# Transposing the first two chunks of x with ordinary matmuls into float32 instead of transposes, and three constant matmuls behind them

## The chip, the cores and the metric

The kernel runs on one core of a Trainium2 chip. The metric is the device time of one execution in microseconds (us). A profile also gives the span, from the program's first to its last instruction on the core. In 13 of the 14 profiles below the measured time is 2.0 to 2.1 us longer than the span, so the two can be read together; the exception is named where it comes.

Engines in the profile lines: PE is TensorE's matmuls, PEld its weight loads, DVE VectorE, ACT ScalarE, SP SyncE; SPq and ACTq are the sequencers that issue transfers.

## The reference

```python
B, S, D, F = 32, 32, 1024, 3584          # all bf16
def reference(x, w_gate, w_up, w_down):
    return (gelu_tanh(x @ w_gate) * (x @ w_up)) @ w_down
```

x is 1024 tokens by 1024; the gate and up weights are 1024 by 3584; the down weight is 3584 by 1024.

## The kernel before

A helper records every operation with its dependencies, so all instructions carry one line number (L117) and one goes by tiles. The first products need x with D on the partitions, in eight chunks of 128 rows (`xT[0][:, k, :]`, 512 tokens each). Chunks 0 and 1 are loaded plainly and transposed by TensorE; chunks 2 to 7 come through the transfer engines' transposing path. Eight matmuls of ones run meanwhile, so that TensorE's clock is up when data arrives.

```python
one = nc.const_aps.tensor(1.0, [P, 512], BF16)
...                                             # ident: the 128x128 identity, bf16
for n in [512] * 6 + [P] * 2:                   # warm-up, bank 3, never read
    mm(3, one[:, 0:P], one[:, 0:n], True, True)
NX = 2                                          # chunks transposed on TensorE
for i, eng in enumerate(("sp", "act")):
    dma(eng, xn[:, 2 * i:2 * i + 2, :], x_r[:, 2 * i:2 * i + 2, 0:NX * P], 0, f"xn{i}")
for k in range(NX):
    load_first("sp", 0, k, k + 1)               # gate weights of chunk k, 128 KB
    load_first("act", 1, k, k + 1)              # up weights
for k0, k1 in ((2, 3), (3, 4), (4, 5), (5, 6), (6, 8)):
    load_x(0, k0, k1)                           # transposing transfer of x, on SP's queue
for k in range(2, 4):
    load_first("act", 0, k, k + 1)
    load_first("act", 1, k, k + 1)
act(warm[:, 0:1], const0, GELU, 0)
for k in range(NX):
    for i, b in enumerate((6, 7) if k == 0 else (4, 5)):
        half = ps[:, b, 0:P].bitcast(BF16)
        for t in range(2):
            pr.add("pe", "transpose", half[:, t * P:(t + 1) * P], xn[:, 2 * i + t, k * P:(k + 1) * P], ident[:, :])
        pr.add("dve", "tensor_copy", xT[0][:, k, i * 256:(i + 1) * 256], half)
...
steps = [(m, j, k) for k in range(DK - KO) for j in range(2) for m in range(4)]   # 8 matmuls a chunk
...
    op = mm(2 * m + j, first[:, j, k, m * P:(m + 1) * P], xT[0][:, k, :], k == 0, k in (3, DK - 1), add=k > 3)
```

Each chunk feeds eight matmuls of 512 columns: four with gate weights, then four with up weights. "The first real matmul" below is the first of chunk 0; the 17th is the first that needs chunk 2. The first GELU on a result runs at about 16 us.

## Time and profile before

| | before |
|---|---|
| time, median of the first 3 runs | 273.2 us (272.43 to 273.35) |
| span of the profiled run | 271.2 us |
| TensorE busy | 267.6 us, 99% |
| first real matmul | 4.61 us |
| slow stretch: 512-column matmuls 0.43 us apart | until 6.3 us; 0.216 us apart afterwards |

The page's engine row and its chain that ended last:

```profile
PE 267.6 (99%) x1197; PEld 191.8 (71%) x1206; DVE 203.5 (75%) x238; ACT 132.8 (49%) x213; POOL 37.2 (14%) x23
...
PE 99%; issue 0%; DVE 0%
PE ps L117 99%; DVE o L117 0%
```

TensorE hardly rests after its start, so whatever the head loses or wins reaches the end. The timeline of the head, TensorE (start us, duration us, engine, line, operation, out<-in, shape, count):

```profile
0.77 2.93 PE L117 MATMUL ps<-const-bfloat16-1.0 128*128 128x512 bf16 x8 [0.77 <-PEq L608]
3.50 1.06 PE L117 MATMUL ps<-ident,hT 128*128 128x128 bf16 x8
4.61 11.56 PE L117 MATMUL ps<-arena 128*128 128x512 bf16 x48
```

The three lines are ones, transposes (the profile calls them matmuls too) and real matmuls. Inside the second, the transposes start 0.107 us apart, the last at 4.25 us; about 0.25 us are then empty before 4.61. The copies on VectorE, from the same timeline:

```profile
3.96 0.93 DVE L117 COPY arena<-ps 128x256 bf16<-128x256 bf16 x4 [3.96 <-PE ps L117]
```

They start 0.215 us apart and take 0.29 us; the second completes chunk 0 at 4.46, and the first real matmul follows 0.15 us later.

The clock has to be read from how many matmuls fit into a microsecond. The stretches view (from:to, length, TensorE busy with the count of matmuls touched, clock column, transfer share, GB/s):

```profile
5.00:6.00 1.00, 1.00 (x4) 1.00 1.22 211
6.00:7.00 1.00, 1.00 (x6) 1.00 1.12 206
7.00:8.00 1.00, 1.00 (x6) 1.00 1.25 201
```

Busy is 1.00 in every row and the clock column says full speed, but only four matmuls touch the first stretch. The Trainium skill, "TensorE: Matmul & The Clock Gate", Part 1, explains it: TensorE starts at half clock, and a free-running activity window of about 3.4 us releases it. The trace agrees on the ratio: 0.43 us a matmul against 0.216. "Release" below means that step. Ten of the 14 traces also keep a record of the clock's steps, which the views do not show; a release given to 0.01 us is read from there. In the other four (the two of the changed kernel, `gap_xfree`, `consts_rep`) it is read from the spacing of the matmuls.

Last, the transfer of x chunk 2, issued at 2.22 us (last column: us from issue to landing):

```profile
arena<-in_x_dram SPq DMA_TRANSPOSE x1, 5.3
```

It lands at 7.54 us; the 17th matmul, which needs it, starts at 8.88. There are 1.3 us to spare here.

### The profile page before, as it was taken

How to read it: one execution, taken by the hardware profiler on the slowest of the kernel's cores; microseconds unless marked ns; L12 is line 12 of the kernel's file. 1: busy time of each engine (PE TensorE's matmuls, PEld its weight loads, DVE VectorE, ACT ScalarE, POOL GpSimd, SP SyncE). 2: the span in 40 equal slices, each digit the busy share in tenths (PEclk: the TensorE clock that was granted, in tenths of full speed). 3: DMA queues.
4: the chain of work that ended last, by engine and by line, in shares of the span. 5: the costliest groups of instructions: out<-in, count | busy, mean ns of one | idle time of the engine just before them, and what ended most of it. 6: DMA issues, size and time to landing. Idle time of an engine off the chain costs nothing.

```text
span 271.2 us, 3314 instructions
## 1 busy us (share of the span) xinstructions
PE 267.6 (99%) x1197; PEld 191.8 (71%) x1206; DVE 203.5 (75%) x238; ACT 132.8 (49%) x213; POOL 37.2 (14%) x23
## 2 busy tenths in 40 slices
PE   8999999999999999999999999999999999999996
PEld 4444448888888888888776776664458888888884
DVE  1341998998899889988764739289976999999911
ACT  2335776566756675667455564531220305067452
POOL 1000003023302330234345060000000000000000
PEclk9999999999999999999999999999999999999999
DMA  7999960050492500942900070293010000002102
GB/s 189 275 282 186 276 187 4 9 147 0 120 294 53 155 0 2 282 145 65 248 0 0 0 259 14 81 347 117 0 39 19 4 0 0 0 0 80 58 19 97
DMA packets 47039, 27.46 MB, mean 101 GB/s; under 512 B 8624, under 2 KB 47024, under 8 KB 47024
## 3 DMA queue, kind: packets, MB, share of 16 engines
q1 hardware_dynamic: 44800, 25.30, 34.4%
q10 hardware_dynamic: 2224, 1.97, 2.8%
q8 instruction: 9, 0.15, 0.2%
q14 instruction: 6, 0.05, 0.1%
HBM read 23.33 MB, written 2.10 MB: 94 GB/s over the span
## 4 chain that ended last, share of the span: by engine, by line
PE 99%; issue 0%; DVE 0%
PE ps L117 99%; DVE o L117 0%
## 5 line engine op out<-in xcount | busy, mean ns | idle before, releaser
L117 PE MATMUL ps<-S,T 128*128 128x512 f32 x560 | 129.2, 391 | 0.0
L117 PEld LDWEIGHTS ps<-S,T 128*128 128x128 f32 x560 | 105.1, 188 | 22.5
L117 ACT ACTIVATE tmp<-ps 128x512 f32<-128x512 f32 x64 | 38.0, 595 | 52.2 <-PE ps L117 52.2
L117 POOL TENSOR_TENSOR T<-arena 128x1024 fp32r<-128x1024 bf16 x17 | 36.5, 2156 | 124.4 <-PE ps L117 74.2
L117 PE MATMUL ps<-T,S 128*128 128x512 f32 x224 | 51.3, 390 | 0.0
L117 DVE TENSOR_TENSOR T<-arena,T 128x1024 fp32r<-128x1024 bf16 x42 | 50.9, 1218 | 0.2
L117 PEld LDWEIGHTS ps<-T,S 128*128 128x128 f32 x224 | 42.0, 188 | 8.8
L117 DVE TENSOR_TENSOR hT<-tmp,ps 128x512 bf16<-128x512 f32 x56 | 37.2, 684 | 14.3 <-PE ps L117 11.9
L117 ACT ACTIVATE ps<-ps 128x512 f32<-128x512 f32 x44 | 25.6, 583 | 36.6 <-PE ps L117 36.6
L117 PE MATMUL ps<-arena 128*128 128x512 bf16 x186 | 42.6, 384 | 0.4
L117 DVE TENSOR_TENSOR tmp<-ps,tmp 128x512 f32<-128x512 f32 x28 | 19.4, 692 | 23.2 <-PE ps L117 23.2
L117 PEld LDWEIGHTS ps<-arena 128*128 128x128 bf16 x192 | 17.8, 98 | 24.3 <-issue 3.2
L117 DVE TENSOR_TENSOR T<-arena 128x1024 fp32r<-128x1024 bf16 x25 | 30.0, 1220 | 5.0 <-PE ps L117 4.3
L117 DVE TENSOR_TENSOR ps<-ps,tmp 128x512 f32<-128x512 f32 x32 | 22.2, 695 | 3.0 <-PE ps L117 3.0
L117 PE MATMUL ps<-arena,hT 128*128 128x512 bf16 (+2 forms) x124 | 24.3, 355 | 0.1
L117 PEld LDWEIGHTS ps<-arena,hT 128*128 128x128 bf16 x126 | 11.7, 98 | 12.7 <-issue 0.5
L117 ACT ACTIVATE tmp<-tmp 128x512 f32<-128x512 f32 x28 | 17.6, 633 | 2.4 <-DVE tmp L117 2.1
L117 DVE TENSOR_TENSOR S<-hT 128x1024 fp32r<-128x1024 bf16 x14 | 16.6, 1219 | 0.0
L117 ACT ACTIVATE T<-arena 128x1024 fp32r<-128x1024 bf16 x14 | 14.8, 1059 | 0.0
L117 ACT ACTIVATE ps<-hT 128x512 f32<-128x512 f32 x18 | 10.7, 599 | 8.0 <-DVE hT L117 8.0
L117 ACT ACTIVATE hT<-ps 128x512 f32<-128x512 f32 x14 | 8.0, 599 | 10.8 <-PE ps L117 10.8
L117 PE MATMUL ps<-S 128*128 128x512 f32 x56 | 12.9, 389 | 0.0
(32 smaller groups left out, 89.1 us busy)
## 6 DMA issues: line engine op xcount, KB each, us to landing
arena<-in_w_down_dram SPq DMA_DIRECT2D x4, 1792.0 KB, 8.8
arena<-in_w_gate_dram SPq DMA_DIRECT2D x10, 512.0 KB, 4.0
arena<-in_w_up_dram SPq DMA_DIRECT2D x10, 512.0 KB, 5.4
out_dram<-arena SPq DMA_DIRECT2D x12, 128.0 KB, 1.7
arena<-in_w_gate_dram SPq DMA_DIRECT2D x4, 256.0 KB, 5.0
arena<-in_w_up_dram SPq DMA_DIRECT2D x4, 256.0 KB, 5.1
arena<-in_w_up_dram ACTq DMA_DIRECT2D x4, 128.0 KB, 4.0
arena<-in_w_gate_dram ACTq DMA_DIRECT2D x2, 256.0 KB, 4.0
```

The lines of the kernel that those rows point to most:

```text
L117: ins = name(eng, *args, **kw) if callable(name) else getattr(eng, name)(*args, **kw)
```

## The change

The intent is to make the head's transposes count as ordinary matmul work for the clock, and to leave TensorE no empty time while VectorE copies. The ordinary matmul writes float32 into PSUM here, so the copies now read float32.

```diff
             for i, b in enumerate((6, 7) if k == 0 else (4, 5)):
-                half = ps[:, b, 0:P].bitcast(BF16)
                 for t in range(2):
-                    pr.add("pe", "transpose", half[:, t * P:(t + 1) * P], xn[:, 2 * i + t, k * P:(k + 1) * P], ident[:, :])
-                pr.add("dve", "tensor_copy", xT[0][:, k, i * 256:(i + 1) * 256], half)
+                    pr.add("pe", "matmul", ps[:, b, t * P:(t + 1) * P], xn[:, 2 * i + t, k * P:(k + 1) * P], ident[:, :], start=True, stop=True)
+                pr.add("dve", "tensor_copy", xT[0][:, k, i * 256:(i + 1) * 256], ps[:, b, 0:256])
+        for n in range(3):
+            mm(3, one[:, 0:P], one[:, 0:P], True, True)
```

## The prediction

> **What bounds the kernel.** TensorE: busy 267.6 of 271.2 us on the page, and 99% of the chain that ended last. Any shift of the head goes one to one into the end.
>
> **The head in the timeline.** Eight matmuls of ones start at 0.77 us, 0.43 us apart (512 columns). From 3.50 the eight transposes start every 0.107 us; the last starts at 4.25. The first real matmul starts at 4.61; about 0.25 us lie idle. That start is set by VectorE: the four copies PSUM to SBUF (128x256 bf16, 0.292 us each, a new one every 0.215 us) begin at 3.96; the second, which completes x chunk 0, ends at 4.46, and 0.15 us later the matmul starts. The gate weights landed at about 4.3, before that. The real matmuls then start 0.43 us apart until 6.3 us, afterwards 0.216: the only slow-clock stretch. (The page's clock row says full speed throughout.)
>
> **What the change does.**
> 1. Transposes become ordinary 128-column matmuls. Two of the 128-column ones matmuls and the transposes show the same spacing, 0.107 us: cost 0.
> 2. The copies now read float32. The trace's 128x512 float32 copy takes 0.684 us, every 0.603; its bf16 256 copy advances 0.215. Taking one element per 0.96 GHz cycle (Trainium skill, "VectorE: DVE Perf Modes", section on PSUM operands: fp32 stays at 1x), I estimate 0.417 us each, every 0.336. Copy 2 then ends at 3.96+0.336+0.417=4.71; first real matmul at about 4.86 instead of 4.61: a loss of 0.25 us, all critical. Chunk 1 is ready at 5.4, needed after 6.5: free.
> 3. Three constant matmuls, 0.107 us each, end issue at about 4.68, inside that wait: cost 0.
> 4. The clock. Trainium skill, "TensorE: Matmul & The Clock Gate", Part 1, says a free-running activity window of about 3.4 us releases the full clock, and Part 4 that transpose mode does not count as busy the same way. In the trace the release came 5.5 us after the first matmul, with 0.86 us of transposes and 0.25 us of gap inside. If those 1.1 us count after the change, release could come up to 1.1 to 1.3 us earlier; at half rate that saves 0.55 to 0.65 us. Against it: the last 3.4 us before the release held the transposes, so they may not have hindered. I give a real effect one chance in two: about -0.3 us on average.
>
> Because the window is free-running, its phase moves single runs by up to 1.7 us (estimate: half of 3.4); runs of before already spread from 272.43 to 273.35, three of four near the top, so some return to the mean is likely (-0.3 us).
>
> Sum: 273.2 + 0.25 - 0.3 - 0.3 = **272.8 us**, range 272.0 to 273.5. Chances: faster by over 2% 0.01, within 2% 0.98, slower by over 2% 0.01.
>
> **What would show it.** Copies of 128x256 at about 0.42 us from a float32 source, against 0.292; first real matmul at 4.8 to 4.9; constants at 0.107 us spacing behind the eighth transpose; the step from 0.43 to 0.216 us spacing at about 5.1 to 5.5 (clock effect) or still 6.3 (none); afterwards both timelines the same, offset by a constant.
>
> **What would make it wrong.** The clock's release depending on something else than counted work (phase alone), float32-source copies as fast as bf16, or chunk 2 and later x and weights, whose transfers land only 1 to 1.5 us before use, becoming the gate when the clock rises earlier.

## The result, and the profile after

| | before | after |
|---|---|---|
| time, median of 6 runs | 273.11 us (272.43 to 273.75) | 273.19 us (272.72 to 273.78) |
| ratio after to before | | 1.0006, 95% interval 0.9985 to 1.0028 |
| span of the profiled run | 271.2 us | 271.6 us |

Ratios are the mean time of one kernel's fast runs over that of the other's in the same rounds, so not quite the ratio of the medians quoted. The later sets were run on three chips, so times compare best within a set. The change makes no measurable difference.

The profile after, first the page's chain that ended last:

```profile
PE 96%; DMA 3%; SPq 0%; issue 0%; DVE 0%
PE ps L117 96%; DMA arena<-in_x_dram 3%; SPq L117 0%; DVE o L117 0%
```

A transfer of x has entered the chain. The timeline of the head, TensorE:

```profile
0.77 2.93 PE L117 MATMUL ps<-const-bfloat16-1.0 128*128 128x512 bf16 x8 [0.77 <-PEq L609]
3.57 1.08 PE L117 MATMUL ps<-ident,hT 128*128 128x128 bf16 x8
4.45 0.53 PE L117 MATMUL ps<-const-bfloat16-1.0 128*128 128x128 bf16 x3
4.91 3.69 PE L117 MATMUL ps<-arena 128*128 128x512 bf16 x16
9.33 6.85 PE L117 MATMUL ps<-arena 128*128 128x512 bf16 x31 [0.73 <-DMA arena<-in_x_dram]
```

The constants sit behind the transposes at 0.107 us spacing and end before the first real matmul, which now starts at 4.91 us, 0.30 later. The first 16 real matmuls take 3.69 us, and then TensorE stands still until x chunk 2 is there: the start of the 17th is 0.89 us later than the 0.216 us spacing would have it. (The bracket says 0.73, because it counts from the modelled end of the matmul before; the waits below are all counted by starts.) The copies:

```profile
4.00 1.42 DVE L117 CAST arena<-ps 128x256 bf16<-128x256 f32 x4 [4.00 <-PE ps L117]
```

One takes 0.42 us and they start 0.33 to 0.34 us apart, as estimated; the second ends at 4.76. The stretches of a microsecond show the clock:

```profile
5.00:6.00 1.00, 1.00 (x5) 1.00 1.38 165
6.00:7.00 1.00, 1.00 (x7) 1.00 0.79 140
7.00:8.00 1.00, 1.00 (x6) 1.00 1.21 177
8.00:9.00 1.00, 0.60 (x3) 1.00 1.31 200
```

The clock is up from about 5.0 us instead of 6.3, but at 8 to 9 us TensorE is only 60% busy. And the transfer of chunk 2, issued at the same 2.22 us:

```profile
arena<-in_x_dram SPq DMA_TRANSPOSE x1, 7.0
```

It landed at 9.19 us instead of 7.54. At full clock the 17th matmul would have wanted it at about 8.4. So this profile shows an earlier clock, a later first matmul, and a new wait that took back more than the clock gave. Which of these belong to the change, and which to the single run, is what the experiments had to say.

### The profile page after: what moved, and what is told of

The parts are those of the page before. It is cut to its first block, busy times and chain, and to the rows that moved or that the text cites. A ratio compares the mean times of both kernels' runs of the same rounds, so it can differ in the third digit from the quotient of the medians.

```text
span 271.6 us, 3329 instructions
## 1 busy us (share of the span) xinstructions
PE 267.9 (99%) x1209; PEld 191.7 (71%) x1209; DVE 204.0 (75%) x238; ACT 132.8 (49%) x213; POOL 37.1 (14%) x23
## 4 chain that ended last, share of the span: by engine, by line
PE 96%; DMA 3%; SPq 0%; issue 0%; DVE 0%
PE ps L117 96%; DMA arena<-in_x_dram 3%; SPq L117 0%; DVE o L117 0%
```

## The experiments

Twelve runs were made, two of them the kernels before and after once more and two of one kernel. Each leaves one profile; most were also timed again, which gives 4 or 6 times in all. At first there were two theories on the clock: A, transposes count less than matmuls towards the release; B, they count alike and the phase of the window decides. Theory C was about the wait: the head runs into the transfer of x, which levels what the clock and the copies give or take.

### Does transpose mode hold the clock back?

The warm-up of the kernel before was filled with transposes, and in a control with ordinary matmuls of the same size.

```diff
-        for n in [512] * 6 + [P] * 2:
+        for n in [512] * 2:
             mm(3, one[:, 0:P], one[:, 0:n], True, True)
+        for n in range(18):
+            pr.add("pe", "transpose", ps[:, 3, 0:P // 2].bitcast(BF16), one[:, 0:P], ident[:, :])   # warm_tr
+            mm(3, one[:, 0:P], ident[:, :], True, True)                                             # warm_mm instead
```

> The kernel before, with the last four 512-column and the two 128-column warm-up matmuls of ones replaced by 18 transposes of 128 columns (same time at the slow clock, 1.93 us), results never read. Theory A (transposes count less towards the release of the full clock than matmuls): the step from 0.43 to 0.216 us spacing moves from 6.3 us to 6.8 us or later, and the kernel takes about 0.5 to 1.5 us longer than before. Rival B (transposes count as matmuls do, the release time is only the phase of a free-running window): the step stays between 3.0 and 6.4 us and the time stays within 0.5 us of before.

> Control for the run with 18 transposes: the same 18 slots filled by ordinary 128-column matmuls against the same identity. Both theories: step in the clock between 3.0 and 6.4 us, time within 0.5 us of before. If this one is also late, small matmuls as such or the data, not transpose mode, hold the clock back.

The timeline of the run with transposes, then that of the control:

```profile
1.58 2.13 PE L117 MATMUL ps<-ident,const-bfloat16-1.0 128*128 128x128 bf16 x18
3.69 1.03 PE L117 MATMUL ps<-ident,hT 128*128 128x128 bf16 x8
4.77 11.59 PE L117 MATMUL ps<-arena 128*128 128x512 bf16 x48
```

```profile
1.58 2.12 PE L117 MATMUL ps<-ident,const-bfloat16-1.0 128*128 128x128 bf16 x18
3.50 1.06 PE L117 MATMUL ps<-ident,hT 128*128 128x128 bf16 x8
4.60 11.64 PE L117 MATMUL ps<-arena 128*128 128x512 bf16 x49
```

The 18 take the same time in both forms. The trace's clock record puts the release at 6.44 us with transposes and at 6.47 with matmuls, one profile each. With transposes the time is 273.55 us, ratio 1.0007 (0.9983 to 1.0031). Theory A expected 6.8 us or later and 0.5 to 1.5 us more. It falls: from 1.58 to 4.5 us nothing but transposes ran, and the release was not later than in the control.

The control's time, 274.3 us (ratio 1.0035, 1.0008 to 1.0061), missed the expectation. Its profiled run took 274.89 us at a span of 271.3, so 3.6 us lie outside the span where nearly all other runs have 2.0 to 2.1; a second of its four runs shows the same (274.81 at 271.2) and a third 2.7 us. The program on the core was not longer: its four spans average 271.25 us, as do the eleven of before in the same set. What the extra time was stays open.

### The same two kernels again

> The changed kernel once more, unedited. Theory A: the step in the clock is at 4.5 to 5.2 us again, earlier than in the kernel before; first real matmul at 4.85 to 4.95 us; and TensorE waits at the 17th real matmul (chunk 2) for the transfer of x whenever that lands after 8.4 us. Rival B: the step lies anywhere between 3.0 and 6.4 us. The landing of x chunk 2 tells a third thing apart: if it is again near 9.2 us the change delays it, if it scatters between 7.5 and 9.2 it is a matter of the single run.

> The kernel before once more, unedited, for a second profile. Theory A: step in the clock at 5.5 to 6.4 us again. Rival B: anywhere between 3.0 and 6.4 us. First real matmul at 4.6 us; x chunk 2 lands between 7.5 and 9.2 us if its landing varies from run to run.

The changed kernel, again: 273.28 us median of 6, ratio 1.0 (0.9983 to 1.0017). Its release came before the first real matmul at 4.90 us; chunk 2 landed at 8.31, chunk 3 at 10.32, and TensorE lost 0.09 and 0.28 us to the two. The kernel before, again (one run, state unknown, 273.34 us); its timeline:

```profile
3.62 1.03 PE L117 MATMUL ps<-ident,hT 128*128 128x128 bf16 x8
4.71 3.89 PE L117 MATMUL ps<-arena 128*128 128x512 bf16 x16
8.93 7.32 PE L117 MATMUL ps<-arena 128*128 128x512 bf16 x33 [0.33 <-DMA arena<-in_x_dram]
```

This is the unchanged kernel, and it shows what I had taken for the mark of the change: release at 4.82 us (clock record), 16 real matmuls in 3.89 us, then the wait for chunk 2, which landed at 8.79. Both the early clock and the late transfer occur without the change, and theory A, which expected 5.5 to 6.4 us here, missed.

### The wait for x taken away

Chunks 2 and 3 read x chunks 0 and 1. The result is wrong; every load and instruction is kept.

```diff
-            op = mm(2 * m + j, first[:, j, k, m * P:(m + 1) * P], xT[0][:, k, :], k == 0, ...)
+            op = mm(2 * m + j, first[:, j, k, m * P:(m + 1) * P], xT[0][:, k - 2 if k in (2, 3) else k, :], k == 0, ...)
```

> The changed kernel, with the matmuls of chunks 2 and 3 reading x chunks 0 and 1 (wrong result on purpose; every load and instruction is kept), so that they no longer wait for the crossbar transfers of x. Theory C (the change's head runs into the transfer of x chunk 2, and whatever the early clock or the copies give or take is levelled there): no wait at the 17th and 25th real matmul, the 61st real matmul starts at 17.8 to 18.1 us instead of 18.2 to 18.8, span 270.6 to 270.9, time 0.2 to 0.6 us under the changed kernel's. Rival D (the wait at chunk 2 costs nothing, something later gives the time back): waits go, but the 61st matmul and the span stay where they were.

> The same edit in the kernel before. Theory C: where the clock is released early (about 4.8 us) the 61st real matmul starts at about 17.7 us, 0.8 us sooner than the 18.46 of the repeat of before; where it is released late (6.3 us) the matmuls were never waiting for x and nothing changes, 18.4 to 18.6 us. The same edit leaves the kernel before ahead of the changed kernel by about 0.3 us at equal release, which is the delay of the first real matmul by the slower copies. Rival D: no difference between the kernels.

The changed kernel with this edit: 272.71 us median (272.49 to 272.96), ratio to before 0.9986 (0.9970 to 1.0002). Its timeline from the first real matmul on:

```profile
4.93 11.38 PE L117 MATMUL ps<-arena 128*128 128x512 bf16 x52 [0.26 <-DVE arena L117]
```

No wait, 61st real matmul at 17.88 us, first GELU at 15.92, span 270.7: as theory C expected. In this profile chunk 2 landed at 7.84 us, though, so it would not have waited anyway; the edit shows in the six times, which are the narrowest of the sets of six and lie 0.57 us under the changed kernel's repeat (of another set on another chip, so only roughly comparable; against before in its own set the interval of the ratio still holds 1).

The kernel before with this edit: 272.94 us median, ratio 0.9999 (0.9979 to 1.0019), but in two groups: 272.60, 272.67, 272.76 and 273.12, 273.62, 273.75. Its profile, of the run at 273.62, has the release at 5.62 us and then another wait:

```profile
4.64 8.40 PE L117 MATMUL ps<-arena 128*128 128x512 bf16 x36
13.54 2.76 PE L117 MATMUL ps<-arena 128*128 128x512 bf16 x12 [0.50 <-DMA arena<-in_w_up_dram]
```

Here the up weights of chunks 4 and 5, which land at 13.49 us, hold TensorE for 0.67 us. Freeing x alone does not free the head: the weights come next. The 61st matmul started at 18.73 us; the expected 17.7 was not seen here, and of a lead over the changed kernel the medians show nothing, the release being late here and early there.

### The constants, alone and taken away

> The changed kernel without the three constant matmuls. Theory C: they lie inside the wait for the copies and the transposes count as activity already, so first real matmul at 4.90 us as with them, time within 0.5 us. If the constants keep the clock, the release falls later than the 4.9 to 5.0 us of both profiles of the changed kernel, at about 6.3 us.

> The kernel before with the three constant matmuls added behind its transposes and nothing else. First real matmul 0.05 to 0.1 us later than 4.60 us (the constants end issue at about 4.68), time within 0.5 us of before. If the constants bring the release of the clock forward, it is at 4.8 to 5.0 us here; if it is the phase alone, 4.8 or 6.3 as chance has it.

`no_consts` is the changed kernel without its last two added lines; `consts_only` is the kernel before with only these two. Without constants: 273.32 us, ratio 1.0006 (0.9986 to 1.0025), first real matmul 5.04 us and not the 4.90 expected, because the plain load of x landed 0.13 us later than in the profile after (3.66 against 3.53) and the transposes with it; release 6.22:

```profile
5.04 11.31 PE L117 MATMUL ps<-arena 128*128 128x512 bf16 x49 [0.30 <-DVE arena L117]
```

```profile
5.00:6.00 1.00, 0.96 (x3) 1.00 1.20 207
```

Constants only: 272.8 us, ratio 0.9992 (0.9969 to 1.0015), first real matmul 4.61 us, so they cost nothing here, and release 4.45, while the constants ran:

```profile
4.35 0.39 PE L117 MATMUL ps<-const-bfloat16-1.0 128*128 128x128 bf16 x3
4.61 11.60 PE L117 MATMUL ps<-arena 128*128 128x512 bf16 x53
```

Its profile is the fastest of all, span 270.4: early release, and x landed at 7.34, so no wait and the 61st real matmul at 17.55 us, 0.32 before `after_xfree`, the changed kernel with an early release and no wait.

By then all four profiles with the constants had a release by about 5.0 us, and only one of six without. From this came theory E: the gap of 0.25 us ahead of the first real matmul delays the release, and the constants close it. Its rival F: the ordinary matmuls do it. With the x edit, so that the times tell the release:

> The kernel before plus the three constant matmuls (transposes and bf16 copies kept), with chunks 2 and 3 reading x chunks 0 and 1 (wrong result on purpose), so that no transfer of x hides the clock: then the time of every run tells when the clock was released. Theory E (the idle gap of 0.25 us ahead of the first real matmul is what puts the release off in many runs; the constants close it, the form of the transpose does not matter): release before 5.0 us in the profile, all runs within about 0.5 us of each other, median 272.2 to 272.6 us, below the 272.71 of the changed kernel with the same edit because the first real matmul starts 0.3 us sooner. Rival F (ordinary matmuls for the transposes release the clock, the constants do nothing): runs scatter over 1 us or more as in the kernel before with this edit (272.6 to 273.75), median near 272.9.

> The changed kernel without the three constants (ordinary matmuls and float32 copies kept), with the same x edit. Theory E: the gap is open, so late releases (5.5 us or more) are back in a good part of the runs: times scatter by 0.7 us or more, upper ones 273.3 to 274.0, median 273.0 to 273.6. Rival F: release before 5.0 us, all runs within 0.5 us, median 272.7 like the changed kernel with this edit.

> The kernel before with the x edit and three needless copies on VectorE ahead of the first one, so that TensorE idles about 0.9 us instead of 0.25 before the first real matmul, which starts at about 5.25 us. Theory E: the release comes late in nearly all runs, 6.0 us or later in the profile, and the runs agree more closely than with the small gap: about 273.4 to 274.2 us. If a gap does not matter and only the phase does: early releases stay about as frequent as in the kernel before, and the lowest runs are at 272.6 + 0.65 = 273.25 us or less.

The third adds copies in front of the first one, to widen the gap:

```diff
+                for d in range(3 if k == 0 and i == 0 else 0):
+                    pr.add("dve", "tensor_copy", tmp[:, 5 + d, 0:P].bitcast(BF16), half)
                 pr.add("dve", "tensor_copy", xT[0][:, k, i * 256:(i + 1) * 256], half)
```

Constants with transposes: 273.06 us median, ratio 0.9998 (0.9980 to 1.0015), the six times in two groups, 272.69, 272.75, 272.79 and 273.34, 273.44, 273.50. The profile is of the run at 273.44; its timeline and its stretches:

```profile
4.47 0.53 PE L117 MATMUL ps<-const-bfloat16-1.0 128*128 128x128 bf16 x3
4.79 11.57 PE L117 MATMUL ps<-arena 128*128 128x512 bf16 x48
```

```profile
5.00:6.00 1.00, 1.00 (x3) 1.00 1.09 176
6.00:7.00 1.00, 1.00 (x5) 1.00 1.11 221
```

The constants are in place, the gap is closed, and only three matmuls touch the stretch from 5 to 6 us: the release was at 6.43. Here, on the slow clock, the constants were not quite free: the first real matmul waited for the last of them and started 0.21 us after the copy, 0.06 more than in every other profile. The kernel with the wide gap, 273.16 us median (272.98 to 273.62), ratio 1.0002 (0.9986 to 1.0018), does the opposite:

```profile
5.19 11.17 PE L117 MATMUL ps<-arena 128*128 128x512 bf16 x50 [0.63 <-DVE arena L117]
```

```profile
5.00:6.00 1.00, 0.81 (x4) 1.00 1.18 228
6.00:7.00 1.00, 1.00 (x6) 1.00 1.25 214
```

TensorE idled for 0.83 us, and yet from its first real matmul on it ran 0.216 us apart: the release came before 5.2 us. Theory E falls on both. The changed kernel without constants (273.23 us median, ratio 1.0004, 0.9985 to 1.0023) has times from 272.73 to 273.90 and a release at 6.69, so ordinary matmuls do not make an early release either, and F falls too. (E forecast this scatter as well, but B forecasts the same.) What is left is B: early or late as chance has it.

The clock record holds one more figure that speaks for B. In all ten traces that have it, the clock falls back to half 266.24 us after its release, the same to 0.001 us, although the last matmul ends anywhere from 1.98 to 3.61 us before that fall. Neither step keeps a fixed distance from the work, but they keep one from each other, as if both lay on a time grid that the program does not set. That such a grid alone decides the release is not shown, as no run sets its phase.

The last run was the constants alone once more, as a correct kernel:

> The kernel before plus only the three constants, correct, once more for its time. Theories C and E: release before 5.0 us, first real matmul 4.6 to 4.7 us, then a wait of 0 to 0.8 us for x chunk 2 as its landing has it; median 272.6 to 273.1 us, 0.2 to 0.5 us below before (about 0.1%), the best correct version of the set. If it equals before, the early clock is spent waiting for x in most runs.

It took 273.11 us (272.56 to 273.45), ratio 0.9998 (0.9980 to 1.0016): release early, first real matmul 4.68 us, and 0.25 and 0.19 us lost to x chunks 2 and 3. The release came among the head's transposes, which take 0.84 us here and 1.03 or more in the other heads with transposes:

```profile
3.60 0.84 PE L117 MATMUL ps<-ident,hT 128*128 128x128 bf16 x8
```

The head was as forecast, but the time, 0.2 to 0.5 us below before, was not. No correct version of the set beats the kernel before by more than the noise.

### The account of all fourteen heads

From the 14 traces: the start of the first real matmul; the time that real matmuls lost to the slow clock (what their spacings exceed 0.216 us by, up to and with the one in which the release falls; a 0.22 us wait for weights in the second profile of before is counted under waits); the waits (larger spacings later, where a spacing of exactly two matmuls is a missing record); the start of the first GELU; and two remainders.

| kernel | first real | release | slow | waits | first GELU | GELU less first, slow, waits | span less GELU |
|---|---|---|---|---|---|---|---|
| before | 4.61 | 6.31 | 0.82 | 0 | 16.42 | 10.99 | 254.8 |
| before, again | 4.71 | 4.82 | 0.04 | 0.77 | 16.50 | 10.99 | 254.8 |
| after | 4.91 | about 5.0 | 0.08 | 0.89 | 16.86 | 10.99 | 254.8 |
| after, again | 4.90 | before first real | 0 | 0.37 | 16.26 | 10.98 | 254.8 |
| warm_tr | 4.77 | 6.44 | 0.81 | 0.25 | 16.82 | 10.99 | 254.8 |
| warm_mm | 4.60 | 6.47 | 0.90 | 0 | 16.50 | 10.99 | 254.8 |
| after_xfree | 4.93 | 4.20 | 0 | 0 | 15.92 | 10.99 | 254.7 |
| before_xfree | 4.64 | 5.62 | 0.47 | 0.68 | 16.77 | 10.99 | 254.8 |
| no_consts | 5.04 | 6.22 | 0.57 | 0 | 16.60 | 10.99 | 254.8 |
| consts_only | 4.61 | 4.45 | 0 | 0 | 15.60 | 10.99 | 254.8 |
| consts_xfree | 4.79 | 6.43 | 0.82 | 0.01 | 16.61 | 10.99 | 254.8 |
| noconsts_xfree | 5.08 | 6.69 | 0.78 | 0.01 | 16.86 | 10.99 | 254.8 |
| gap_xfree | 5.19 | before first real | 0 | 0 | 16.17 | 10.99 | 254.8 |
| consts_rep | 4.68 | before first real | 0 | 0.44 | 16.10 | 10.98 | 254.8 |

The last two columns are constant: 10.98 to 10.99 and 254.7 to 254.8 us. So every difference between these spans, 270.4 to 271.6 us, is the sum of three terms: when the first real matmul starts, how long it then runs on half clock, and how long the head waits for transfers. Only the first of them is shown to be set by the change, and that in part. From the start of the first transpose to the first real matmul it is 1.08 to 1.11 us in the seven heads with bf16 copies and neither a widened gap nor late constants, and 1.33 to 1.34 in the five with float32 copies: 0.22 to 0.26 us for the copies. The rest is when the transposes start, 3.50 to 3.74 us: 0.05 us after the plain load of x on SP's queue lands, or at 3.50, right behind the ones, where it lands before.

Two things follow for the comparison. The difference of the first pair of spans (0.4 us) is 0.30 for the later first matmul, less 0.75 for the clock, plus 0.89 for the wait, 0.44 in all, as between the two GELU starts. And the terms work against each other: with a late release TensorE is too slow to need x early, and a later first real matmul loses fewer slow matmuls (`no_consts` against before: 0.43 us later, 0.26 us less slow time); with an early release it can run ahead to the transfer, and where it does, a later start only shortens the wait.

## Why the prediction was right

The time was predicted at 272.8 us, 272.0 to 273.5, within 2% at 0.98; 273.19 was measured. Point by point:

1. TensorE bounds the kernel and the head's shift goes one to one into the end: right. Span less first GELU is 254.7 to 254.8 us in all 14 profiles.
2. Transposes cost the same in either form: right, 0.107 us apart on the slow clock in both.
3. Float32 copies at 0.417 us, one every 0.336: measured 0.42 and 0.33 to 0.34. First real matmul at about 4.86, 0.25 us later: measured 4.90 and 4.91, 0.20 to 0.30 us later than in the two profiles of before, and 0.22 to 0.26 once the start of the transposes is taken out. Right in mechanism; but "all critical" holds only where the release is early and no transfer is late.
4. Constants cost nothing: right for the change, where they end before the copies do. Behind bf16 copies they cost 0 (`consts_only`) and 0.06 us (`consts_xfree`).
5. The clock, -0.3 us on average as a one-in-two effect of counted work: this term is not supported. Filling the warm-up with transposes did not put the release later than matmuls did (6.44 against 6.47 us), a wide gap did not keep it from coming early (before 5.2 us with 0.83 us idle), and closing the gap did not keep it from coming late (6.43 us with constants). The release scatters from about 4.1 to 6.69 us over the 14 profiles, with transposes from 4.1 to 6.47 and with ordinary matmuls in their place from 4.20 to 6.69. Whether the change shifts the odds stays open: five of six profiles with the constants released by about 5.0 us and two of eight without (the wide gap counted as early), which is suggestive, but with the x edit the six times of the constants split three to three, while the six of the changed kernel all lie close together and low.
6. Return to the mean, -0.3 us: too large. From 273.2 us, before went to 273.11 with three more runs, and to 273.28, 273.27 and 272.93 in three sets of eleven, so 0.3 down at most and 0.1 or less, up or down, in the others.
7. The list of what would make it wrong named the transfers of chunk 2 becoming the gate under an earlier clock. That belonged into the sum. Waits for x cost 0 and 0.54 us in the two profiles of before and 0.89 and 0.37 in the two of the changed kernel, and can take back all that an early clock gives.

So the central value was 0.4 us under the measured one. Without terms 5 and 6 the sum would have been 273.45, about 0.3 over it; medians of the unchanged kernel alone ran from 272.93 to 273.28, so the time cannot tell which is nearer. The range held because each term is small beside 273 us. The copies' term was confirmed by the traces; the agreement in time is no test of the clock's term, and to that extent it was luck.

## What to carry to other kernels

Before costing a change to a kernel's head, take several profiles of the unchanged kernel, whose times alone ran from 272.43 to 274.31 us here: one profile of each version showed an "early clock" and a "new transfer wait" as if the change had made them, and the second profile of the old kernel showed both. Split the head into terms whose remainder is constant from run to run (here first real matmul, slow clock, waits), so that chance and change come apart. And a head that is fed just in time has no single limit: what the clock gives, the next transfer can take, so speeding up one of them alone may move the total little.

## What the Trainium skill lacked or had wrong

- "TensorE: Matmul & The Clock Gate", Part 4, says that transpose mode does not count as busy in the same way and that full clock does not engage for it. Here the release came at 6.44 us with a warm-up of 18 transposes, followed by the 8 of the head, and at 6.47 with 18 ordinary matmuls in their place (one profile each), and in the last run (`consts_rep`) transposes went from 0.107 to 0.06 us apart at about 4.1 us: they do run at full clock.
- The same page, Part 1, gives the transition as about 4 us after the start of activity, 0.5 us either way from run to run. Its window of about 3.4 us agrees with the earliest releases here, 3.3 to 3.4 us after the first matmul at 0.77 us (`consts_rep` at about 4.1 and `after_xfree` at 4.20); the latest came 5.9 us after it, a wider scatter than 0.5 us.
- "Perfetto Trace Analysis", Optimizing Tensor Performance, asks that transposes be done as transposes and not as matmuls, because they have logic that skips the arithmetic. On TensorE the two forms took the same 0.107 us on the slow clock; what the matmul form cost here was the float32 copy, 0.34 us apart instead of 0.215. The page does not say so.
- "VectorE: DVE Perf Modes", section on PSUM operands, has float32 from PSUM at 1x and bf16 at up to 2x. Nothing wrong there: the copies agree in direction (0.42 against 0.29 us for 256 elements), at a ratio of 1.4 in duration and 1.6 in spacing.
- No page read here gives the scatter of a transfer's landing: the transposing transfer of x chunk 2, issued at 2.22 us each time, landed anywhere from 7.34 to 9.19 us over the 14 profiles.
